# Unsplit float32 operands in the first block of a linear-attention and two-MLP kernel

## The chip, the cores and the metric

The kernel runs on one core of a Trainium2 chip. The metric is the device time of one execution in microseconds. Five engines work side by side, each through its own queue in order: TensorE (PE; its weight loads are listed as PEld), VectorE (DVE), ScalarE (ACT), GpSimd (POOL) and SyncE (SP), which here issues the DMAs.

## The reference

```python
def _attn_ref(q, k, v):              # 8 batches, 8 heads, 576 rows, 64 columns
    q_s = q - np.max(q, axis=-1, keepdims=True)
    q_s = np.exp(q_s)
    q_s = q_s / (np.sum(q_s, axis=-1, keepdims=True) + 1e-09)
    k_s = k - np.max(k, axis=2, keepdims=True)
    k_s = np.exp(k_s)
    k_s = k_s / (np.sum(k_s, axis=2, keepdims=True) + 1e-09)
    kv = np.einsum('bhsd,bhse->bhde', k_s, v)
    return np.einsum('bhsd,bhde->bhse', q_s, kv).astype(np.float32)

def _moe_ref(x, w_in, w_out):        # x 4608 x 512, w_in 512 x 2048, w_out 2048 x 512
    h = np.maximum(x @ w_in, 0.0)
    return (h * h @ w_out).astype(np.float32)

# the second MLP: h = x @ w_in;  g = h * (1 / (1 + exp(-h)));  g @ w_out
```

The output of the attention, 4608 rows of 512, goes through the first MLP and then through the second. Weights come as 64-bit floats.

## The kernel before, in words

Rows are handled in nine blocks of 512 for the first MLP: one for each batch's first 512 rows, and a ninth from the last 64 rows of all eight batches. The second MLP runs over six blocks of 768 rows.

Most products are made of "split" operands: `split` (L126) copies a float32 value to a rounded float32r part `hi` on ScalarE and subtracts it on VectorE to get `lo`; `mm3` (L195) multiplies hi by hi, hi by lo and lo by hi, three matmuls for one product. A few products use plain float32 operands: `kv` (L306) and the transposes `q_t` (L383).

The attention works on pairs of heads (`Pair`, L211), each in four phases (L434): maxima and exponents; subtraction, exponent of k and normalization of q; the product of k and v (`kvp`), the transposes of q and their split; the product of q with kv (`x`) and its evacuation. Batches 0 and 1 (`by_chunk = 2`, `natural`) lay rows out by chunk and reduce k over a strided axis (L279); the others use VectorE's transposes. Batch 0 is done before everything else (L716 to L760), its results split into `x0` at L424. The other batches are spread over the later work, one phase each time `next(attend)` is called.

The first block of the first MLP (L769 to L790) runs over 16 chunks f of the hidden width. In each, `h_mm` (L660) makes the first product of chunk f + 1 from `x0` and the weights of pair f // 2, `relu2` (L653) turns it into `g`, one attention phase is emitted, and `out_mm` (L672) adds chunk f to the second product `op`. Beside it the weights are converted from 64-bit words to float32 in `to_f32` (L146: two ScalarE and four VectorE operations) and split (`split_w`, L167), one half of a pair in each round: `o == 0` is the half of w_in, `o == 1` that of w_out. The float32 form of w_in is also stored (L174) for later.

The other eight blocks use Strassen-like products (`strassen`, L613): seven products per pair of chunks, of a left factor `wah`, `wal` (made by `make_wa`, L498, from the stored weights: a load, four VectorE operations, a split of 1792 columns, two stores) with seven combinations of x (class `X`, L540). A `Cache` (L473) holds two left factors; `want(t)` makes or loads those of the next uses. The first two are made at f = 14 (L782), followed by x of block 1.

Tiles of 8 KB per partition come from 19 shared slots through `take` and `give` (L81 to L90), oldest free slot first. A planner orders each engine's instructions ahead of time by its own estimates, so neighbouring steps are interleaved; `keep_in_program_order` keeps an instruction from moving ahead of earlier ones of its engine.

Of the kernel before, what the change touches and what calls it, by code (L numbers as in the profile page):

```python
# [10 lines left out]
F32 = mybir.dt.float32  # L11
F32R = mybir.dt.float32r
# [19 lines left out]
def kernel(  # L32
# [25 lines left out]
    NQ = 7  # L58
    TS = 768
    TH = TS // 2  # L60
    assert SM == TB and B * SL == TB and NB == B + 1 and SL <= P

    NP = NF // 2
    NS = 19
# [16 lines left out]
    def take(shape, dt, name):  # L81

        at = idle.pop(0)
        t = spool.tile(shape, dt, tag=f"s{at}", name=name)
        slot_of[id(t)] = (at, t)
        return t
# [5 lines left out]
    def f32(t):  # L92
        return t.bitcast(F32)
# [32 lines left out]
    def split(hi, lo, src):  # L126
        nc.scalar.copy(hi, src)  # L127
        nc.vector.tensor_sub(lo, src, f32(hi))  # L128
# [37 lines left out]

    def split_w(i, o, raw, pin=False):  # L167

        u = upool.tile([P, PW], U32, tag="u", name="u")
        to_f32(u, raw, pin)  # L170
        give(raw)
        yield
        if o == 0:
            nc.sync.dma_start(out=wf[0, i, o], in_=f32(u))  # L174
        W[i, o] = w = take([P, 2, PW], F32R, "w")
        split(w[:, 0], w[:, 1], f32(u))
        yield
# [17 lines left out]
    def mm3(ps, lh, ll, rh, rl, first, last):  # L195
# [2 lines left out]
        nc.tensor.matmul(ps, ll, rh, start=False, stop=last)  # L198


    x0 = [take([P, NK, TB], F32R, name) for name in ("xh", "xl")]
    XR = {}
    big = {}
    PLACES = {
# [4 lines left out]
    }  # L209

    class Pair:  # L211
# [64 lines left out]

        def k_max(self):
            m = self.tile("m", [P, 2, D], F32)
            r = nc.vector.reduce_max(m, self.kr.rearrange("p a c d -> p a d c"), axis=AX.X)  # L279
            if (self.b, self.p) == (1, 0):  # L280
                tc.keep_in_program_order(r)
            self.m = self.tile("mb", [P, 2, D], F32)
            nc.gpsimd.partition_all_reduce(
                self.m.rearrange("p a d -> p (a d)"), m.rearrange("p a d -> p (a d)"), P, bass_isa.ReduceOp.max
            )
# [28 lines left out]
        def kv_evac(self):  # L314
            rec = self.tile("rec", [P, 1], F32)
            nc.vector.tensor_scalar_add(rec, self.kvp[:, 2 * D:2 * D + 1], 1e-9)
            nc.vector.reciprocal(rec, rec)
            t = self.tile("m" if not self.early else "kvt", [P, 2 * D], F32)
            nc.vector.scalar_tensor_tensor(
                out=t, in0=self.kvp[:, 0:2 * D], scalar=rec, in1=mask_n if self.natural else mask_t,  # L320
                op0=ALU.mult, op1=ALU.mult,
            )
            self.kvh = self.tile("kvh", [P, 2 * D], F32R)
            self.kvl = self.tile("kvl", [P, 2 * D], F32R)
            nc.vector.tensor_copy(self.kvh, t)
            nc.vector.tensor_sub(self.kvl, t, f32(self.kvh))
# [69 lines left out]
                nc.vector.transpose(self.pt, self.q.rearrange("p c d -> p (c d)"))  # L396

        def q_split(self):
            self.qh = self.tile("qh", [P, S], F32R)
            self.ql = self.tile("ql", [P, S], F32R)  # L400
            if self.natural:
                split(self.qh[:, 0:SM], self.ql[:, 0:SM], self.pt[0])
                split(self.qh[:, SM:S], self.ql[:, SM:S], self.pt[1][:, 0:SL])
            else:
                split(self.qh, self.ql, self.pt)

        def x(self):
            ps = []
            for hf in range(2):
                xp = ps_a.tile([P, TB], F32, tag="pa", name="xp")  # L410
                s = slice(hf * HALF, (hf + 1) * HALF)
                mm3(xp[:, 0:HALF], self.kvh, self.kvl, self.qh[:, s], self.ql[:, s], True, True)
                ps.append(xp)
            self.xp = ps

        def x_evac(self):
            p, b = self.p, self.b
            if p == 0 and b > 0:
                XR[b] = take([P, NK, TB], F32, "xr")
            for hf, xp in enumerate(self.xp):  # L420
                n = HALF if hf == 0 else SM - HALF
                t0 = hf * HALF
                if b == 0:
                    split(x0[0][:, p, t0:t0 + n], x0[1][:, p, t0:t0 + n], xp[:, 0:n])  # L424
                else:
                    nc.scalar.copy(XR[b][:, p, t0:t0 + n], xp[:, 0:n])
                if hf == 1:
                    t = self.tile("xe", [P, SL], F32)
                    nc.scalar.copy(t, xp[:, n:n + SL])
                    nc.sync.dma_start(out=xld[p, :, b * SL:(b + 1) * SL], in_=t)  # L430
            if self.early:
                give(*(big[p, i] for i in range(3)))
# [40 lines left out]
    class Cache:  # L473
# [3 lines left out]
            self.n, self.uses, self.make, self.load = n, uses, make, load  # L477
            self.tiles, self.made = {}, set()

        def want(self, t):  # L480
            coming = list(dict.fromkeys(self.uses[t:]))
            for i in coming[:self.n]:
                if i in self.tiles:
                    continue
                if len(self.tiles) == self.n:
                    out = max(self.tiles, key=lambda x: coming.index(x) if x in coming else len(self.uses))
                    give(*self.tiles.pop(out))
                self.tiles[i] = (self.load if i in self.made else self.make)(*i)
                self.made.add(i)
# [170 lines left out]
    def h_mm(f):  # L660
        w = W[f // 2, 0]
        hp = ps_q.tile([P, TB], F32, tag="ac"[f % 2], name="hp")
        for c in range(NK):
            s = slice((f % 2 * NK + c) * P, (f % 2 * NK + c + 1) * P)
            mm3(hp, w[:, 0, s], w[:, 1, s], x0[0][:, c, :], x0[1][:, c, :], c == 0, c == NK - 1)
        if f % 2:
            give(W.pop((f // 2, 0)))
        return hp
# [103 lines left out]
    for f in range(NF):  # L772
        if f % 2 == 0 and f // 2 + 2 < NP:
            for o in range(2):
                raws.append(load_w(0, f // 2 + 2, o))
        if f + 2 < NF:
            run(split_w(f // 2 + 1, f % 2, raws.pop(0), pin=f == 0))
        if f + 1 < NF:
            G[f + 1] = first_g(f + 1)
        next(attend, None)  # L780
        if f == NF - 2:
            wa.want(0)  # L782
            xs = x_first(1)
            xs.split(2)
        elif f == NF - 1:
            give(*x0)
            xs.split(5)
        if f < NF - 2:
            run(out_mm(0, f // 2, f % 2, G.pop(f), f == 0, False))
# [3 lines left out]
    for j in range(1, NB):  # L793
        x, xs = xs, None
        for m, i in enumerate(turns[j - 1]):
            def hook(n):
                if n in (1, 6):
                    next(attend, None)
                    if j == 1 and (m, n) in ((1, 6), (3, 6)):
                        next(attend, None)  # L800
# [133 lines left out]
```

## Time and profile before

| what | us |
|---|---|
| median of 3 runs (lowest, highest) | 1693.26 (1692.67, 1694.72) |
| profiled execution, its own time | 1693.5 |
| its span in the profile | 1691.7 |
| mean granted TensorE clock | 0.994 of full |

Times in rows are microseconds from the start of the span, and mean durations of single instructions nanoseconds. L609 is line 609 of the kernel. A bracket at the end of a row is idle time of that engine just before it, with what ended it. Ends of matmuls are modelled, so the busy time of TensorE includes tails that overlap; the distance from start to start is the cost of one in a stream.

### The profile page before, as it was taken

The numbers are of one execution on the slowest core, as the hardware profiler recorded it, in microseconds if no ns is written. First come the engines' busy times: TensorE is split into PE (matmuls) and PEld (weight loads), VectorE is DVE, ScalarE is ACT, GpSimd is POOL, SyncE is SP. The second block draws the span as 40 slices with busy tenths as digits, with TensorE's granted clock in tenths as the row PEclk, the third lists the DMA queues.
The fourth block names the chain that finished last, engine by engine and source line by source line (L and its number), as shares of the span: only waits on it lengthen the run. The fifth ranks groups of instructions, "written<-read, shape, count | busy, mean of one in ns | idle before, by whom it ended". The sixth has DMA issues, their size and how long they took to land.

```text
span 1691.7 us, 23448 instructions
## 1 busy us (share of the span) xinstructions
PE 1633.6 (97%) x8904; PEld 1436.0 (85%) x8904; DVE 1015.5 (60%) x1723; ACT 868.2 (51%) x1551; POOL 55.5 (3%) x118
## 2 busy tenths in 40 slices
PE   4898999999999999999999999999999999999998
PEld 3676888888888888898988898899889889889887
DVE  7999888686776858653435675434444444444333
ACT  4876566565666656654546544334334334334332
POOL 1000000010101001000000000000000000000000
PEclk8999999999999999999999999999999999999999
DMA  7754667858576785746264875534534534534621
GB/s 210 253 196 159 190 210 220 260 160 256 177 236 193 208 242 166 250 146 237 109 215 171 332 280 196 188 131 167 196 132 158 196 141 149 196 150 149 218 94 38
DMA packets 193504, 320.31 MB, mean 189 GB/s; under 512 B 113264, under 2 KB 142960, under 8 KB 188528
## 3 DMA queue, kind: packets, MB, share of 16 engines
q1 hardware_dynamic: 193392, 318.81, 57.0%
q8 instruction: 70, 1.15, 0.3%
q14 instruction: 42, 0.34, 0.1%
HBM read 248.51 MB, written 70.25 MB: 188 GB/s over the span
## 4 chain that ended last, share of the span: by engine, by line
PE 72%; DVE 11%; ACT 5%; DMA 5%; issue 5%; SPq 1%; POOL 0%; POOLq 0%; DVEq 0%; ACTq 0%
PE a L609 18%; PE c L609 14%; PE y L197 8%; PE y L198 8%; PE y L196 8%; PE op L197 4%; PE op L196 4%; PE op L198 4%; DMA raw<-in_moe_w_out_dram 2%; DMA raw<-in_moe_w_in_dram 2%; PE kvp L310 1%; DVE u L160 1%; DVE g L128 1%; DVE u L163 1%; ACT raw L152 1%
## 5 line engine op out<-in xcount | busy, mean ns | idle before, releaser
L609 PE MATMUL a<-x,wah 128*128 128x256 f32 (+1 forms) x1792 | 398.0, 309 | 8.7 <-ACT h L646 4.4
L609 PEld LDWEIGHTS a<-x,wah 128*128 128x128 f32 x1792 | 314.9, 189 | 54.6 <-ACT h L646 9.7
L609 PE MATMUL c<-x,wah 128*128 128x256 f32 (+1 forms) x1344 | 296.3, 307 | 2.4 <-ACT h L624 1.8
L609 PE MATMUL a<-x,wal 128*128 128x256 f32 (+1 forms) x896 | 275.4, 307 | 0.6 <-DVE wal L128 0.5
L609 PEld LDWEIGHTS c<-x,wah 128*128 128x128 f32 x1344 | 237.9, 189 | 33.8 <-ACT h L624 3.8
L197 PE MATMUL op<-g,w 128*128 128x512 f32 x576 | 230.0, 399 | 2.9 <-DVE g L128 2.1
L196 PE MATMUL op<-g,w 128*128 128x512 f32 x576 | 224.2, 398 | 6.3 <-ACT g L127 3.9
L198 PE MATMUL y<-wb,g 128*128 128x512 f32 x576 | 227.2, 394 | 0.0
L197 PE MATMUL y<-wb,g 128*128 128x512 f32 x576 | 227.1, 394 | 0.0
L198 PE MATMUL op<-g,w 128*128 128x512 f32 x576 | 224.7, 392 | 0.0
L196 PE MATMUL y<-wb,g 128*128 128x512 f32 x576 | 223.5, 389 | 0.0
L609 PE MATMUL c<-x,wal 128*128 128x256 f32 (+1 forms) x672 | 206.6, 307 | 0.0
L870 ACT ACTIVATE z<-h 128x768 f32<-128x768 f32 x96 | 81.1, 846 | 227.8 <-DVE h L641 226.5
L632 DVE TENSOR_TENSOR h<-c,h 128x256 f32<-128x256 f32 (+1 forms) x112 | 53.6, 479 | 224.0 <-PE c L609 221.5
L609 PEld LDWEIGHTS a<-x,wal 128*128 128x128 f32 x896 | 169.3, 189 | 1.5 <-DVE wal L128 1.4
L654 ACT ACTIVATE h<-h 128x512 f32<-128x512 f32 x128 | 80.7, 630 | 119.9 <-DVE h L641 119.3
L128 DVE TENSOR_TENSOR g<-h,g 128x512 fp32r<-128x512 f32 x128 | 88.2, 690 | 78.2 <-ACT g L127 78.0
L871 DVE TENSOR_TENSOR z<-z,h 128x768 f32<-128x768 f32 x96 | 91.7, 957 | 68.5 <-ACT z L870 68.5
L198 PEld LDWEIGHTS y<-wb,g 128*128 128x128 f32 x576 | 107.9, 187 | 23.3
L609 PEld LDWEIGHTS c<-x,wal 128*128 128x128 f32 x672 | 127.2, 189 | 0.4
L198 PEld LDWEIGHTS op<-g,w 128*128 128x128 f32 x576 | 108.3, 188 | 21.7
L128 DVE TENSOR_TENSOR g<-z,g 128x768 fp32r<-128x768 f32 x96 | 91.6, 954 | 56.1 <-ACT g L127 56.1
(148 smaller groups left out, 2350.6 us busy)
## 6 DMA issues: line engine op xcount, KB each, us to landing
wah<-wad SPq DMA_DIRECT2D x72, 896.0 KB, 6.5
wal<-wad SPq DMA_DIRECT2D x72, 896.0 KB, 6.2
wb<-wbd SPq DMA_DIRECT2D x30, 1024.0 KB, 4.8
raw<-in_moe_w_in_dram SPq DMA_DIRECT2D x32, 512.0 KB, 5.3
raw<-in_moe_w_out_dram SPq DMA_DIRECT2D x32, 512.0 KB, 5.2
wad<-wah SPq DMA_DIRECT2D x16, 896.0 KB, 3.6
wad<-wal SPq DMA_DIRECT2D x16, 896.0 KB, 4.6
wf<-u SPq DMA_DIRECT2D x24, 512.0 KB, 4.9
```

The lines of the kernel that those rows point to most:

```text
L128: nc.vector.tensor_sub(lo, src, f32(hi))
L152: first = nc.scalar.activation(f32(lo32), lo32, AF.Copy, scale=2.0 ** -51, bias=2.0)
L160: nc.vector.scalar_tensor_tensor(out=u, in0=hi32, scalar=0x80000000, in1=u, op0=ALU.bitwise_and, op1=ALU.bitwise_xor)
L163: nc.vector.tensor_tensor(out=u, in0=u, in1=lo32, op=ALU.add)
L196: nc.tensor.matmul(ps, lh, rh, start=first, stop=False)
L197: nc.tensor.matmul(ps, lh, rl, start=False, stop=False)
L198: nc.tensor.matmul(ps, ll, rh, start=False, stop=last)
L609: nc.tensor.matmul(ps, l, r, start=first and c == 0 and n == 0, stop=c == 1 and n == 2, skip_group_check=True)
L632: nc.vector.tensor_add(h[:, 0, two], c, h[:, 0, two])
L654: nc.scalar.activation(h, src, AF.Relu)
L870: nc.scalar.activation(z, h, AF.Sigmoid)
L871: nc.vector.tensor_mul(z, z, h)
```

## The change

Four edits. In batches 0 and 1 the q and kv operands are not split: kv stays in one float32 tile, the transposed q is copied to one float32 tile, and each half of `x` is one float32 matmul. The results of batch 0 go unsplit to `XR[0]`, as those of the other batches do. Of the weights in the first block, those of w_in are converted into a shared slot and used unsplit by `h_mm`, one float32 matmul for each of four chunks in place of three of split operands; w_out is split as before. The k maxima of batches 0 and 1 are made by three `tensor_max` in place of one reduction. The first left factor is made at f = 12, the second inside the first Strassen block ahead of its fourth product.

```diff
@@ split_w
-        u = upool.tile([P, PW], U32, tag="u", name="u")
+        u = take([P, PW], U32, "w32") if o == 0 else upool.tile([P, PW], U32, tag="u", name="u")
         to_f32(u, raw, pin)
         give(raw)
         yield
         if o == 0:
             nc.sync.dma_start(out=wf[0, i, o], in_=f32(u))
+            W[i, o] = u
+            return
         W[i, o] = w = take([P, 2, PW], F32R, "w")
@@ before Pair
-    x0 = [take([P, NK, TB], F32R, name) for name in ("xh", "xl")]
-    XR = {}
+    XR = {0: take([P, NK, TB], F32, "xr")}
@@ Pair.k_max
-            r = nc.vector.reduce_max(m, self.kr.rearrange("p a c d -> p a d c"), axis=AX.X)
+            if self.natural:
+                t = self.tile("km", [P, 2, 2, D], F32)
+                nc.vector.tensor_max(t, self.kr[:, :, 0:2], self.kr[:, :, 2:4])
+                nc.vector.tensor_max(t[:, :, 0], t[:, :, 0], t[:, :, 1])
+                r = nc.vector.tensor_max(m, t[:, :, 0], self.kr[:, :, 4])
+            else:
+                r = nc.vector.reduce_max(m, self.kr.rearrange("p a c d -> p a d c"), axis=AX.X)
@@ Pair.kv_evac
+            if self.natural:
+                self.kv32 = t
+                return
             self.kvh = self.tile("kvh", [P, 2 * D], F32R)
@@ Pair.q_split
+            if self.natural:
+                self.q32 = self.tile("qh", [P, S], F32)
+                nc.scalar.copy(self.q32[:, 0:SM], self.pt[0])
+                nc.scalar.copy(self.q32[:, SM:S], self.pt[1][:, 0:SL])
+                return
@@ Pair.x
-                mm3(xp[:, 0:HALF], self.kvh, self.kvl, self.qh[:, s], self.ql[:, s], True, True)
+                if self.natural:
+                    nc.tensor.matmul(xp[:, 0:HALF], self.kv32, self.q32[:, s], start=True, stop=True)
+                else:
+                    mm3(xp[:, 0:HALF], self.kvh, self.kvl, self.qh[:, s], self.ql[:, s], True, True)
@@ Pair.x_evac
-                if b == 0:
-                    split(x0[0][:, p, t0:t0 + n], x0[1][:, p, t0:t0 + n], xp[:, 0:n])
-                else:
-                    nc.scalar.copy(XR[b][:, p, t0:t0 + n], xp[:, 0:n])
+                nc.scalar.copy(XR[b][:, p, t0:t0 + n], xp[:, 0:n])
@@ Cache
-        def want(self, t):
+        def want(self, t, n=None):
-            for i in coming[:self.n]:
+            for i in coming[:n or self.n]:
@@ h_mm
-            mm3(hp, w[:, 0, s], w[:, 1, s], x0[0][:, c, :], x0[1][:, c, :], c == 0, c == NK - 1)
+            nc.tensor.matmul(hp, f32(w[:, s]), XR[0][:, c], start=c == 0, stop=c == NK - 1)
@@ loop over f
-        if f == NF - 2:
-            wa.want(0)
+        if f == NF - 4:
+            wa.want(0, 1)
+        elif f == NF - 2:
             xs = x_first(1)
             xs.split(2)
         elif f == NF - 1:
-            give(*x0)
+            give(XR.pop(0))
@@ hook(n) of the Strassen blocks
+                if (j, m, n) == (1, 0, 3):
+                    wa.want(0)
```

## Rows read from the trace of the kernel before

**Rows 1.** The page: busy time of each engine and its share of the span.

```profile
PE 1633.6 (97%) x8904; PEld 1436.0 (85%) x8904; DVE 1015.5 (60%) x1723; ACT 868.2 (51%) x1551; POOL 55.5 (3%) x118
```

**Rows 2.** Busy by stretch: length, PE, PEld, DVE, ACT, POOL (instructions), clock, DMA, GB/s.

```profile
20.30:55.10 34.80, 26.94 (x108) 19.90 (x108) 30.55 (x67) 24.33 (x68) 1.16 (x3) 0.85 0.70 214
55.10:152.60 97.50, 91.94 (x414) 71.19 (x414) 95.23 (x139) 71.86 (x103) 9.96 (x15) 1.00 0.61 196
152.60:180.00 27.40, 21.55 (x100) 17.34 (x99) 25.43 (x50) 16.91 (x32) 1.01 (x3) 0.81 0.58 203
...
200.00:1691.70 1491.70, 1473.52 (x8163) 1310.23 (x8161) 835.98 (x1414) 736.88 (x1314) 36.26 (x64) 1.00 0.57 188
```

**Rows 3.** Busy time in three periods of the loop, kvp to kvp.

```profile
61.60:85.90 24.30, 22.85 (x105) 18.34 (x106) 24.07 (x38) 21.76 (x32) 3.24 (x4) 1.00 0.83 265
85.90:114.80 28.90, 26.88 (x121) 20.61 (x120) 27.72 (x38) 23.33 (x33) 2.99 (x4) 1.00 0.62 208
114.80:144.40 29.60, 28.12 (x127) 21.88 (x127) 28.98 (x41) 17.95 (x27) 2.72 (x4) 1.00 0.31 101
```

**Rows 4.** TensorE in order of time: start, length, instruction; ten starts, 58.80 to 60.90.

```profile
22.29 1.50 PE L310 MATMUL kvp<-big 128*128 128x129 f32 x6
...
29.04 0.83 PE L310 MATMUL kvp<-big 128*128 128x129 f32 x6
...
58.80 0.40 PE L198 MATMUL op<-g,w 128*128 128x512 f32 x1
...
60.90 0.40 PE L198 MATMUL op<-g,w 128*128 128x512 f32 x1
```

**Rows 5.** Line 310, 21.9 to 31.8 us: durations in ns, least, median, most.

```profile
L310 PE MATMUL kvp<-big x30: 272/422/583, 21.9 to 30.1; 128*128 128x129 f32 x24, 64*128 64x129 f32 x6
```

**Rows 6.** Groups of instructions, 0 to 200 us: busy us, mean ns, idle before.

```profile
L279 DVE TENSOR_REDUCE m<-kr 128x128 f32<-128x640 f32 x7 | 9.2, 1314 | 0.0
...
L127 ACT CAST wah<-c 128x1792 fp32r<-128x1792 f32 x4 | 6.8, 1693 | 2.2 <-DVE c L506 2.2
...
L338 DVE TENSOR_REDUCE qm<-q 128x10 f32<-128x640 f32 x4 | 3.2, 812 | 0.0
...
L128 DVE TENSOR_TENSOR ql<-qt,qh 128x512 fp32r<-128x512 f32 x4 | 2.8, 691 | 0.6 <-ACT qh L127 0.5
...
L326 DVE TENSOR_TENSOR kvl<-m,kvh 128x128 fp32r<-128x128 f32 x6 | 1.7, 284 | 0.0
...
L503 DVE TENSOR_TENSOR c<-c 128x256 f32<-128x256 f32 x4 | 1.6, 412 | 0.0
```

**Rows 7.** VectorE in order of time, start of the kernel.

```profile
36.16 0.45 DVE L128 TENSOR_TENSOR xl<-xp,xh 128x288 fp32r<-128x288 f32 x1
36.52 1.21 DVE L128 TENSOR_TENSOR w<-u,w 128x1024 fp32r<-128x1024 f32 x1
37.65 0.22 DVE L325 CAST big<-big 128x128 fp32r<-128x128 f32 x1
38.91 0.69 DVE L128 TENSOR_TENSOR big<-qt,big 128x512 fp32r<-128x512 f32 x1 [1.04 <-ACT big L127]
...
43.45 0.46 DVE L128 TENSOR_TENSOR xl<-xp,xh 128x288 fp32r<-128x288 f32 x1 [1.95 <-ACT xh L127]
```

**Rows 8.** TensorE in order of time, the first second product.

```profile
55.14 1.20 PE L196 MATMUL op<-g,w 128*128 128x512 f32 x4 [2.25 <-ACT g L127]
```

**Rows 9.** VectorE in order of time, change of stage.

```profile
157.25 2.02 DVE L128 TENSOR_TENSOR wal<-c,wah 128x1792 fp32r<-128x1792 f32 x1
...
161.33 0.68 DVE L128 TENSOR_TENSOR x<-xr,x 128x512 fp32r<-128x512 f32 x1
161.93 2.01 DVE L128 TENSOR_TENSOR wal<-c,wah 128x1792 fp32r<-128x1792 f32 x1
```

**Rows 10.** TensorE in order of time, the first Strassen product.

```profile
162.07 0.38 PE L609 MATMUL a<-x,wah 128*128 128x256 f32 x1 [1.79 <-DVE x L128]
```

**Rows 11.** SP's waits, 0 to 200 us: total, times, longest.

```profile
SPq L511 <- ACT wah L127: 6.1, 3, 2.3
```

More of the change, by code (lines that the diff above doesn't have):

```diff
@@ L60 @@
     TH = TS // 2
-    assert SM == TB and B * SL == TB and NB == B + 1 and SL <= P
+    assert SC == 4 and SM == TB and B * SL == TB and NB == B + 1 and SL <= P
     NP = NF // 2
@@ L398, in q_split @@
         def q_split(self):
+            if self.natural:
[3 more added lines that the diff above has]
+                return
             self.qh = self.tile("qh", [P, S], F32R)
             self.ql = self.tile("ql", [P, S], F32R)
-            if self.natural:
-                split(self.qh[:, 0:SM], self.ql[:, 0:SM], self.pt[0])
-                split(self.qh[:, SM:S], self.ql[:, SM:S], self.pt[1][:, 0:SL])
-            else:
-                split(self.qh, self.ql, self.pt)
+            split(self.qh, self.ql, self.pt)
         def x(self):
@@ L422, in x_evac @@
                 t0 = hf * HALF
-                if b == 0:
-                    split(x0[0][:, p, t0:t0 + n], x0[1][:, p, t0:t0 + n], xp[:, 0:n])
-                else:
-                    nc.scalar.copy(XR[b][:, p, t0:t0 + n], xp[:, 0:n])
+                nc.scalar.copy(XR[b][:, p, t0:t0 + n], xp[:, 0:n])
                 if hf == 1:
```

4 rows, old and new, of the table PLACES are left out of this document.

## The prediction

> **What bounds the kernel now.** I read the busy table of the page first, then the stretches of the first 200 us, then single instructions. TensorE is busy 97% of the span [rows 1], but that busy time includes its modelled pipeline tails, so I look for the stretches where it is not fed. There are three [rows 2]: 20.3 to 55.1 us (the attention of batch 0 and the first conversion; TensorE 26.9 of 34.8 us busy, mean clock 0.85), 55.1 to 152.6 us (the loop over f, 14 rounds of one first product and one second product), and 152.6 to 180 us (the change to the Strassen blocks; 21.6 of 27.4 us, clock 0.81). Behind 200 us TensorE is fed (1473.5 of 1491.7 us) and the change removes nothing, so I price that stretch at 0; the shared tile slots rotate in another order there, for which I keep 2 us on either side.
>
> In the loop VectorE, not TensorE, sets the pace. One period of four rounds (one head pair of attention, four weight conversions) took 28.9 and 29.6 us in the second and third period, with VectorE busy 27.7 and 29.0 us [rows 3]. TensorE's own work in a period is smaller. A split product of 512 columns starts every (60.90 - 58.80)/9 = 0.23 us [rows 4], so a round's 12 + 12 of them are 5.52 us, four rounds 22.1. A head pair adds ten kvp instructions at (0.83 - 0.272)/5 = 0.111 us [rows 4, 5], with a restart between chunks about 1.25; five transposes of the same rate, 0.55; and six xp matmuls of 288 columns at 0.13, scaled from the 512 (0.8). Together 24.7 us: 4 to 5 us of each late period are waits.
>
> **The change part by part, float32 on TensorE.** In the trace one float32 matmul in the code is two instructions: ten kvp for the five chunks. At full clock they start 0.111 us apart, at half clock (1.50 - 0.42)/5 = 0.216 us [rows 4, 5] (one lasts 0.27 or 0.42 us); for 129 columns that is two column times each (258 cycles of 1.2 GHz are 0.215 us). A second reading is one column time plus 128 columns of weights; 129 columns can't tell the two apart. Against it: the split products also load 128 weight columns for each matmul, and at 0.23 us for 512 columns (0.213 at one per cycle) nearly nothing of that shows. I take two column times per instruction: 512 columns cost 0.43 us, a chunk 0.86, a first product 4 x 0.86 = 3.45 us where 12 x 0.23 = 2.76 stood. Bounds for one first product: 2.13 us (the second reading, 8 x 640 columns) and 3.52 (8 x 512/129 x 0.111). The Trainium skill (FP8 and Floating Point Precision, TensorE Precision Notes) counts four passes for true FP32, which speaks against trading three split passes for it; by that rule the product is 3.4 us, by the second reading 2.1, and no run here yet shows float32 at 512 columns.
> Two float32 xp matmuls are 4 x 0.245 = 1.0 us for 0.8. A period of TensorE becomes 4 x (3.45 + 2.76) + 1.25 + 0.55 + 1.0 = 27.6 us.
>
> **VectorE and ScalarE relief.** Consecutive instructions overlap by about 0.08 us (a 1.21 us subtraction starts 1.13 us before the next [rows 7]), so I take means less 0.08 [rows 6]. Out of a period go: two weight subtractions 2 x 1.13 = 2.26; the q subtractions 0.61 + 0.14 (the 64-column one by the 128-column kvl less a third); kvl 0.20 and its copy, 0.13 by the same row; and 0.49 of the k maxima (the strided reduction 1.23, in its place one 256-element operation 0.33 and two of 128 at 0.20). That is 3.83 us, leaving 24 to 25 of 28 to 29. ScalarE loses two casts per period and is no bound (71.9 of 97.5 us [rows 2]).
> For the maxima the trace decides against a rule. The strided reduction takes 1314 ns, a reduction of as many elements along the row 812 [rows 6]: the layout costs 0.5 us, and it leaves with the reduction. The Trainium skill (VectorE: DVE Perf Modes, The TRN2 errata) says each small instruction pays its fixed part again. By its formula for two-operand adds, (N + 151)/0.96, taken for all four, one 640-element operation is 0.82 us and the three 1.01, an estimated loss of 0.2 per pair where the rows give a gain of 0.49.
>
> **The loop, 55.1 to 152.6.** After the change TensorE (27.6) is over VectorE (24 to 25), so TensorE bounds it: 3.5 periods are 96.6 us, and I add 3 us of waits. The nearest row for that is the first period, in which VectorE still had conversions done ahead: 24.3 us for about 24.7 of TensorE work [rows 3]. Sum 99.6 against 97.5: **+2**. Bounds: -0.5 (0.4 of waits) and +10 (today's 97.5 - 3.5 x 24.7 = 11 of waits stay).
>
> **The start, 20.3 to 55.1.** For the four pairs of batch 0 and the first weights VectorE loses 4 x (0.49 + 0.75 + 0.33), the subtractions of x (4 x 0.66: 0.36 by the starts at 36.16 and 36.52 [rows 7], and 0.3 for the shorter half) and one weight subtraction 1.13: 10.1 us. With them go its waits on ScalarE's copies, 1.04 and 1.95 [rows 7]; the first second product now starts at 55.14 after 2.25 us of waiting for g [rows 8]. If all of VectorE's time is on the path the gain is 13 us. TensorE gets 2 x 0.69 + 0.8 = 2.2 us more, partly at half clock, and the second conversion is emitted one round earlier, where ScalarE can stand before its data (0 to 3 us), so the other bound is +2. VectorE is busy 30.6 of 34.8 us [rows 2], which is nearer to the full gain, but the loads, TensorE and the chain through pair 3 share the path: I take half, **-6**.
>
> **The change of stage, 152.6 to 180.** Two left factors are made here now, each one 512 KB load, four VectorE operations (4 x 0.34), a ScalarE cast (1.69), a VectorE subtraction (1.94) and two 896 KB stores [rows 6, 9]. Both subtractions (157.25, 161.93) stand between the operations that make x [rows 9], and TensorE waits for x, 1.79 us at 162.07 [rows 10]. The first factor moves two rounds up: its 3.3 us of VectorE lie under the loop's 3 us per period of new slack; uncovered they would cost 3.3. The second moves behind all of x. Its load and stores stand in SP's order before the k, q and v loads of the pair after next, and SP already stands at such stores (6.1 us in three waits [rows 11]); those loads are used a block later, so I price that at 0, up to 2. The seven splits of x come about 4 us sooner, limited by the attention's output and the four subtractions ahead; TensorE's half-clock stretch behind the wait shrinks, 3; VectorE enters without its backlog, 1; and the second factor then costs its 3.3 us before the second block, of which I count 2. **-6**. Bounds: -12 (all waiting in these 27.4 us) and +9 (below). The POOL maxima stay as they are.
>
> **Sum.** -6 + 2 - 6 = -10 against the profiled execution's own 1693.5 us (span 1691.7, 1.8 around it), which lies 0.2 above the median 1693.26: **1683**.
>
> **The rivals.**
> 1. The waits of the loop stay (+10): they come from the chain from one product through ScalarE and VectorE to the next, not from VectorE's total. For it: at 55.14 TensorE waits for ScalarE's g, not for a busy VectorE. Against: the first period has no such waits. With -6 at the start and -4 at the change of stage it is 1693: no change that can be told.
> 2. Slower: the second factor is late. Place: between the first and second Strassen block, some 165 to 185 us. It can start only when VectorE has left x and the attention in front of it; four operations, cast and subtraction are 1.34 + 1.69 + 1.94 = 5 us in line [rows 6, 9], and if TensorE falls to half clock again, some 8 us of products lose 4 more. Then this stretch is +9 and the sum -6 + 2 + 9 = +5: 1698. It decides from +7.4 on in this stretch. For it: VectorE is busy in nearly all of it; against: TensorE still has second products to fill with.
> 3. Much faster: float32 goes by the second reading (loop back to VectorE's 24 to 25 per period, -10 to -12), or start and change of stage recover nearly all their waiting. 1671.
> 4. The change doesn't show: the planner orders the instructions so that the freed time becomes idle time on VectorE. 1693, counted with 1.
>
> **How the numbers follow.** Forecast 1683 (its own range 1677 to 1689.5): 0.56. Rivals 1 and 4: 0.20. Rival 2: 0.14. Rival 3: 0.10. The measurement can tell about 0.2%, 3.4 us. Faster is the forecast and rival 3: 0.66; same 0.20; slower 0.14. The range leaves out most of rival 2 and the far side of rival 3: 1673 to 1695.
>
> **What would show it.** Right: hp in 128 instructions 0.43 us apart at full clock; the first op near 49 us; periods of 28 to 29 us with VectorE under 26 busy; the first product of the blocks without the 1.8 us wait and its factor stored two rounds before. Wrong: hp spacing near 0.27 (rival 3), periods over 30 (rival 1), TensorE waiting for the second wal behind the first block (rival 2).

## The result

The changed kernel takes 1673.03 us (median of 4 runs, 1669.79 to 1675.97) beside 1692.97 for the kernel before on the same chip: a ratio of 0.9883, 95% interval 0.986 to 0.9905, or 20 us less. The forecast was 1683: faster, as it said, but by twice as much. The time lies at the very edge of the range that was given, 1673 to 1695, and outside the forecast's own, 1677 to 1689.5.

The page of the kernel after, its first line (against [rows 1]), and its granted clock in 40 slices:

```profile
PE 1632.9 (98%) x8824; PEld 1420.0 (85%) x8824; DVE 993.3 (59%) x1691; ACT 861.2 (51%) x1543; POOL 50.8 (3%) x118
...
PEclk9999999999999999999999999999999999999999
```

TensorE is as busy as before (1632.9 and 1633.6 us), in a span that is 17.5 us shorter: what has gone is waits. Busy by stretch, with the columns of [rows 2] (length, PE, PEld, DVE, ACT, POOL with instructions, clock, DMA, GB/s): start, loop over f, first Strassen step, and what lies behind the third:

```profile
17.10:46.10 29.00, 24.75 (x91) 16.57 (x92) 22.41 (x44) 21.96 (x72) 3.85 (x7) 1.00 0.61 180
46.10:149.00 102.90, 99.41 (x354) 61.67 (x353) 95.15 (x151) 72.61 (x105) 6.94 (x15) 1.00 0.72 230
149.00:163.60 14.60, 13.48 (x80) 11.24 (x79) 12.55 (x19) 9.95 (x19) 1.01 (x3) 1.00 0.57 169
...
188.30:1669.40 1481.10, 1470.95 (x8153) 1309.61 (x8153) 831.14 (x1408) 735.46 (x1312) 33.48 (x63) 1.00 0.56 187
```

The start is 6 us shorter and begins 3 us sooner, the loop is 5 us longer, and the change of stage (last first product to the end of the first Strassen step) takes 14.6 us where it took 24.1 (152.6 to 176.7). The clock, 0.85 and 0.81 in two stretches of [rows 2], is 1.00 in all of these (1.00 is 2.4 GHz; the traces show one other level, half of it). Three periods of the loop, as in [rows 3]:

```profile
51.90:83.30 31.40, 30.73 (x104) 18.20 (x103) 31.01 (x46) 25.40 (x36) 1.83 (x5) 1.00 0.84 283
83.30:111.30 28.00, 28.00 (x100) 17.55 (x99) 27.63 (x40) 23.11 (x32) 1.70 (x4) 1.00 0.95 299
111.30:140.90 29.60, 28.09 (x100) 17.55 (x99) 26.17 (x40) 16.36 (x26) 2.40 (x3) 1.00 0.48 158
```

The second and third are 28 and 29.6 us, as forecast. The first, 31.4, is not a period like them: by its instructions it holds 40 of the first product where they hold 32. TensorE in order of time at the first second product, and at the end of the loop:

```profile
42.25 4.46 PE L676 MATMUL hp<-xr,w 128*128 128x512 f32 x10
46.14 1.03 PE L198 MATMUL op<-g,w 128*128 128x512 f32 x2
...
146.41 3.17 PE L676 MATMUL hp<-xr,w 128*128 128x512 f32 x7
149.42 1.13 PE L424 MATMUL xp<-qh,m 128*128 128x288 f32 x4
150.17 0.62 PE L620 MATMUL a<-x,wah 128*128 128x256 f32 x2
```

Seven float32 instructions from 146.41 to 149.42 are 0.430 us each: the price of the forecast's first reading (0.43). The first second product starts without a wait (2.25 us in [rows 8]), and so does the first Strassen product at 150.17. (Before, the row of [rows 10] is that product's second instruction; the first ran at 157.11, and then the product waited 1.79 us for x.) VectorE at the start and at the factors, which are to be set against [rows 9]:

```profile
0.81 0.06 DVE L102 MEMSET tiny<- 128x1 f32 x1 [0.81 <-PEq L932]
3.63 0.42 DVE L282 TENSOR_TENSOR big<-big 128x256 f32<-128x256 f32 x1 [2.76 <-DMA big<-in_k_dram]
4.09 0.29 DVE L283 TENSOR_TENSOR big<-big 128x128 f32<-128x128 f32 x1
6.89 0.42 DVE L282 TENSOR_TENSOR big<-big 128x256 f32<-128x256 f32 x1 [2.51 <-DMA big<-in_k_dram]
7.35 0.29 DVE L283 TENSOR_TENSOR big<-big 128x128 f32<-128x128 f32 x1
11.10 0.29 DVE L284 TENSOR_TENSOR big<-big 128x128 f32<-128x128 f32 x1 [3.45 <-DMA raw<-in_moe_w_in_dram]
...
15.45 0.42 DVE L282 TENSOR_TENSOR big<-big 128x256 f32<-128x256 f32 x1
15.78 0.21 DVE L379 RECIPROCAL big<-big 128x10 f32<-128x10 f32 x1
15.91 0.28 DVE L283 TENSOR_TENSOR big<-big 128x128 f32<-128x128 f32 x1
16.11 0.82 DVE L381 TENSOR_TENSOR qn<-big 128x640 f32<-128x640 f32 x1
...
17.58 0.28 DVE L284 TENSOR_TENSOR big<-big 128x128 f32<-128x128 f32 x1
17.77 0.81 DVE L348 TENSOR_REDUCE big<-big 128x10 f32<-128x640 f32 x1
...
131.81 2.02 DVE L128 TENSOR_TENSOR wal<-c,wah 128x1792 fp32r<-128x1792 f32 x1
...
153.63 2.02 DVE L128 TENSOR_TENSOR wal<-c,wah 128x1792 fp32r<-128x1792 f32 x1
```

For pairs 0 and 1 two of the three maxima now run between 3.63 and 7.64, from the landing of their first part of k on; before, VectorE's first operation on data, a strided reduction, began at 10.43. GpSimd in the kernel before, that reduction, and GpSimd after the change:

```profile
10.19 0.20 POOL L253 MEMSET big<- 64x128 f32 x1
```

```profile
10.43 1.24 DVE L279 TENSOR_REDUCE big<-big 128x128 f32<-128x640 f32 x1 [9.56 <-POOL big L253]
```

```profile
10.86 0.20 POOL L254 MEMSET big<- 64x128 f32 x1
```

The reduction did not wait for a load: both loads of k of pair 0 had landed by 4.05 us. It waited for GpSimd, which fills the padding rows of the fifth chunk of k (L253) only after its masks, until 10.39. The first two maxima don't read that chunk and need not wait for it; the third does, as the reduction did, and starts at 11.10, just behind the memset (the bracket of its row names a load that landed shortly before it). No run moved the memset itself forward, so what that would give is open. The first factor's subtraction stands 25 us sooner than in the kernel before, the second's 8.

### The profile page after: what moved, and what is told of

It is laid out like the page before. It is cut to its first block, busy times and chain, and to the rows that moved or that the text cites. A ratio compares the mean times of both kernels' runs of the same rounds, so it can differ in the third digit from the quotient of the medians.

```text
span 1674.2 us, 23234 instructions
## 1 busy us (share of the span) xinstructions
PE 1632.9 (98%) x8824; PEld 1420.0 (85%) x8824; DVE 993.3 (59%) x1691; ACT 861.2 (51%) x1543; POOL 50.8 (3%) x118
## 4 chain that ended last, share of the span: by engine, by line
PE 62%; DVE 2%; ACT 2%; DMA 2%; issue 1%; POOL 0%; DVEq 0%; POOLq 0%; ACTq 0%; SPq 0%
PE a L620 16%; PE c L620 12%; PE y L199 8%; PE y L200 8%; PE y L198 8%; PE op L199 3%; PE op L198 3%; PE op L200 3%; PE kvp L317 0%; DMA x1d<-o 0%; ACT h L665 0%; DMA raw<-in_moe_w_in_dram 0%; DMA raw<-in_moe_w_out_dram 0%; DMA c<-wf 0%; ACT h L666 0%
## 5 line engine op out<-in xcount | busy, mean ns | idle before, releaser
L620 PEld LDWEIGHTS c<-x,wah 128*128 128x128 f32 x1344 | 237.1, 188 | 31.8 <-ACT h L635 3.1
L200 PEld LDWEIGHTS op<-g,w 128*128 128x128 f32 x576 | 108.3, 188 | 21.9
```

The costliest lines, as they stand in the source:

```text
L620: nc.tensor.matmul(ps, l, r, start=first and c == 0 and n == 0, stop=c == 1 and n == 2, skip_group_check=True)
```

## The experiments

The kernels are compared by their times and by five points of their traces: first transpose (qt), first second product (op), last first product (hp), end of the first and of the third Strassen step; and by the length from there to the last product of the second MLP. Times are medians; ratios are to the kernel before, run beside each.

| kernel | us | ratio, interval | qt | op | last hp | step 1 | step 3 | behind |
|---|---|---|---|---|---|---|---|---|
| before | 1692.97 | 1 | 20.3 | 55.1 | 152.6 | 176.7 | 201.0 | 1486.0 |
| after | 1673.03 | 0.9883, 0.9860–0.9905 | 17.1 | 46.1 | 149.0 | 163.6 | 188.3 | 1481.1 |
| product_only | 1679.56 | 0.9923, 0.9906–0.9941 | 20.8 | 49.9 | 152.4 | 165.4 | 191.2 | 1478.4 |
| qkv_only | 1686.37 | 0.9963, 0.9948–0.9978 | 21.2 | 52.7 | 146.7 | 168.2 | 192.5 | 1485.0 |
| kmax_only | 1692.60 | 1.0003, 0.9991–1.0014 | 16.3 | 51.8 | 149.9 | 173.9 | 198.2 | 1486.5 |
| factor_only | 1697.26 | 1.0034, 1.0021–1.0048 | 20.1 | 54.2 | 151.8 | 174.6 | 200.0 | 1496.7 |
| after_no_factor | 1673.09 | 0.9881, 0.9862–0.9901 | 16.9 | 45.9 | 148.5 | 161.9 | 186.9 | 1482.0 |
| after_no_kmax | 1679.72 | 0.9922, 0.9908–0.9937 | 20.7 | 47.9 | 152.5 | 167.2 | 191.9 | 1481.5 |
| after_no_qkv | 1683.83 | 0.9952, 0.9938–0.9967 | 16.9 | 50.2 | 149.3 | 162.6 | 187.6 | 1488.2 |
| before_pe_more | 1689.45 | 0.9977, 0.9959–0.9996 | 20.7 | 55.2 | 159.0 | 174.0 | 198.3 | 1485.4 |
| before_dve_more | 1699.95 | 1.0052, 1.0034–1.0069 | 21.2 | 55.3 | 162.3 | 185.3 | 209.6 | 1483.6 |
| after_pe_more | 1689.52 | 0.9983, 0.9969–0.9997 | 16.7 | 44.0 | 160.0 | 174.6 | 199.7 | 1478.3 |
| after_dve_more | 1685.18 | 0.9955, 0.9939–0.9971 | 16.2 | 43.4 | 145.5 | 160.1 | 184.4 | 1491.8 |
| before_fill | 1693.22 | 1.0010, 0.9998–1.0023 | 21.1 | 52.5 | 152.8 | 177.2 | 204.2 | 1480.6 |

Runs of one kernel lie up to 2 to 8 us from their median, so a point of one trace is good to a few us. Some traces are of runs at the edge: factor_only's took 1703.2 us, the longest of 12, after_pe_more's 1684.6, the shortest of 10, and the changed kernel's 1676.0, the longest of 4.

### One part alone

**product_only**: the kernel before with the float32 first product and its operands.

```diff
-            mm3(hp, w[:, 0, s], w[:, 1, s], x0[0][:, c, :], x0[1][:, c, :], c == 0, c == NK - 1)
+            nc.tensor.matmul(hp, f32(w[:, s]), XR[0][:, c], start=c == 0, stop=c == NK - 1)
```

> The first block's first product alone in float32 on unsplit operands (weights of w_in and x of block 0 unsplit); q and kv split, k maxima by the reduction, both left factors at f = 14, as before. Theory 1 (VectorE's relief is worth what it frees at the start and at the change of stage, while the loop is given to TensorE): start -4, loop +4 to +6 (14 x 0.69 more TensorE work, VectorE near 26 per period), change of stage -2, in all -2: 1691, between 1688 and 1695. Theory 2 (most of the change's 20 us is TensorE's clock, which stays full once this product no longer waits for VectorE's subtractions): the granted clock is 1.00 through 30 to 60 us, and the time is 1685 or less.

It gave 12 us, not 2 (1679.56 beside 1691.83). What theory 2 asked for came true, a clock of 1.00 through 30 to 60 us and a time under 1685; but VectorE's relief came with it; the section on the clock looks at the clock by itself. The loop is 102.5 us, as after the change, and the change of stage 13.0 with both factors called where they were before. Its loop and first Strassen step:

```profile
49.90:152.40 102.50, 99.15 (x359) 61.73 (x359) 98.11 (x151) 72.04 (x103) 8.75 (x15) 1.00 0.71 234
152.40:165.40 13.00, 12.02 (x78) 10.45 (x77) 12.68 (x29) 9.55 (x20) 1.05 (x3) 1.00 0.32 96
```

The planner had put both subtractions of the left factors into the loop by itself, at 140.6 and 145.3 us, into the time that VectorE no longer needs:

```profile
140.59 2.02 DVE L128 TENSOR_TENSOR wal<-c,wah 128x1792 fp32r<-128x1792 f32 x1
...
145.29 2.02 DVE L128 TENSOR_TENSOR wal<-c,wah 128x1792 fp32r<-128x1792 f32 x1 [0.55 <-ACT wah L127]
```

VectorE has 10.8 us less to do in the change of stage (12.68 for 23.46), and the stretch is 11.1 us shorter. The two factors are about 5 of these; splits of x and work of the attention, which also stand elsewhere now, are the rest.

**qkv_only**: q, kv and `x` of batches 0 and 1 unsplit, nothing else.

```diff
-                mm3(xp[:, 0:HALF], self.kvh, self.kvl, self.qh[:, s], self.ql[:, s], True, True)
+                if self.natural:
+                    nc.tensor.matmul(xp[:, 0:HALF], self.kv32, self.q32[:, s], start=True, stop=True)
+                else:
+                    mm3(xp[:, 0:HALF], self.kvh, self.kvl, self.qh[:, s], self.ql[:, s], True, True)
```

> q with kv alone in float32 in batches 0 and 1; everything else as before. Theory 1: VectorE loses 1.08 us in each of eight pairs, 4.3 at the start and 4.3 in the loop, where it sets the pace, TensorE gains 0.2 per pair: -4 to -7, 1687 to 1690. Theory 2 (clock): less than -2 unless the clock of 30 to 50 us rises.

5.5 us less (1686.37 beside 1691.83), as the sum for this part said: loop 94.0 us (3.5 shorter: TensorE does not bound it here and VectorE has less), start 3.3 shorter, measured from the first transpose.

**factor_only**: `want(0, 1)` at f = NF - 4 and the second `want(0)` in the first Strassen step.

```diff
-        if f == NF - 2:
-            wa.want(0)
+        if f == NF - 4:
+            wa.want(0, 1)
+        elif f == NF - 2:
             xs = x_first(1)
```

> The first left factor at f = 12 and the second inside the first Strassen block; everything else as before. Theory 1 (the move pays only under the loop's slack): 3.3 us of VectorE are added to a loop that VectorE bounds, +3, and 5 are gained at the change of stage: -2, 1691. Theory 3 (the place alone pays: x is no longer behind two factors, TensorE does not wait and its clock does not fall): -6 to -10 with the granted clock 1.00 through 160 to 180 us.

Slower by 5.4 us (1697.26 beside 1691.83), which neither theory had. Up to the third step it is 1.0 us ahead; the loss comes behind, 1496.7 us for 1486.0 (see the last part of this section). Moving the factor in a kernel whose VectorE has no free time before the change of stage moves the end of the first step by 2 us.

**after_no_factor**: the changed kernel with both factors made at f = 14 as before.

```diff
-        if f == NF - 4:
-            wa.want(0, 1)
-        elif f == NF - 2:
+        if f == NF - 2:
+            wa.want(0)
             xs = x_first(1)
```

> The changed kernel with both left factors at f = 14 again. Theory 1: the change of stage is some 5 to 6 us longer than in the changed kernel, 1678 to 1680. Theory 3: 8 to 10 us longer, 1681 to 1683, with the clock falling in 150 to 180 us. If neither (under 2 us): the 10 us at the change of stage came from VectorE entering it without backlog.

1673.09: the move is worth nothing in the change, which is the third case of the expectation (VectorE enters the change of stage without a backlog). The subtractions of both factors stand at 137.0 and 138.9 us without it.

**kmax_only** and **after_no_kmax**: the maxima by halves alone, and the change without them.

```diff
+                nc.vector.tensor_max(t, self.kr[:, :, 0:2], self.kr[:, :, 2:4])
+                nc.vector.tensor_max(t[:, :, 0], t[:, :, 0], t[:, :, 1])
+                r = nc.vector.tensor_max(m, t[:, :, 0], self.kr[:, :, 4])
```

> The kernel before with the maxima of k of the first two batches by halves, alone. Theory of the forecast (0.49 us of VectorE per pair, eight pairs, VectorE being the pace up to 152 us): start 2 us sooner, loop 1 to 2 shorter, time down by 2 to 4. Theory 2 (the first maximum can start when the first half of k has landed, as the trace after the change shows with its first VectorE operation at 3.6 us in place of 10.4): first transpose at 17, down by 4 to 6. By the Trainium skill (VectorE: DVE Perf Modes, The TRN2 errata), which has each small instruction pay its fixed part: up by 0 to 2.

> The changed kernel with the maxima of k by one strided reduction again. Theory 2 (the maxima by halves bring the first transpose 3 us forward): first transpose at 20 to 21, first op at 49, time up by 2 to 5 against the changed kernel (1675 to 1678). Theory of the forecast (only 0.49 us per pair, and the loop is bound by TensorE now): up by 1 to 2.

Alone no change can be told in the time (1692.60 beside 1691.71, where the two theories had 2 to 6 us less; only the third forecast, up by 0 to 2, fits the time), though the trace is 4.0 us ahead at the first transpose and 2.8 at the third step. In the changed kernel the medians differ by 6.7 us, more than any theory said and clear of noise, and the traces by 3.6 at the third step and 4.0 in all. So the edit brings the first transpose forward by 3 to 4 us, of which 3 or so are left at the third step. Why the time shows nothing of it in one kernel and more in the other stays open.

**after_no_qkv**: the change with q and kv split.

```diff
-                self.q32 = self.tile("qh", [P, S], F32)
+                split(self.qh[:, 0:SM], self.ql[:, 0:SM], self.pt[0])
+                split(self.qh[:, SM:S], self.ql[:, SM:S], self.pt[1][:, 0:SL])
```

> The changed kernel with q and kv of batches 0 and 1 split again (two subtractions and one copy more for q and kv of each pair on VectorE, 1.08 us a pair; x by three split matmuls, 0.2 us a pair less on TensorE). Theory 1 (only VectorE's work ahead of the loop still counts, since TensorE is the pace in the loop): first op 2 to 4 us later than 46.1, loop within 2 us of 103, time up by 2 to 4 against the changed kernel (1675 to 1678). Rival (the edit is worth as much here as alone, where it gave 6 us): 1678 to 1681. If TensorE's 0.2 us a pair decides: within 1 us of the changed kernel.

First op 4.1 us later, as theory 1 said (2 to 4), but the loop is 3.8 shorter (99.1), and the third step ends 0.7 sooner than in the changed kernel: the 8.5 us that this part gives alone up to there (201.0 to 192.5) are not to be had a second time once the product has relieved VectorE. The time is 10.8 us longer all the same, more than any of the three expectations, and the trace shows where: it is 7.1 us longer behind the third step.

### Which engine sets the pace of the loop

Four kernels add the same kind of work to before and after. On TensorE the first of the four products of `h_mm` is repeated (its sum is begun anew), once after and four times before the change, about 0.9 us a round; on VectorE the clip of a conversion is repeated (it finds nothing left to clip), 0.61 us a round.

```diff
+            if c == 0 and f:
+                nc.tensor.matmul(hp, f32(w[:, s]), XR[0][:, c], start=True, stop=True)
```

```diff
-        nc.vector.tensor_scalar(
-            out=f32(u), in0=f32(u), scalar1=EXP_LO, scalar2=EXP_HI, op0=ALU.max, op1=ALU.min
-        )
+        for _ in range(1 + more):
+            nc.vector.tensor_scalar(
+                out=f32(u), in0=f32(u), scalar1=EXP_LO, scalar2=EXP_HI, op0=ALU.max, op1=ALU.min
+            )
```

**after_pe_more**

> The changed kernel with more TensorE work in the loop over f and no other: in rounds 1 to 15 the first of the four float32 products of h_mm is issued twice (the second one starts the sum anew), two instructions of 0.43 us, so 0.86 us a round, 12 us over the 14 rounds between the first second product and the last first product. Theory 1 (after the change TensorE is the pace of the loop): that stretch goes from 103 to 112 to 115 us, the time up by 9 to 13. Rival (the pace is still VectorE or the chain through ScalarE and VectorE): stretch up by under 4 us, time up by 0 to 5.

**after_dve_more**

> The changed kernel with more VectorE work in the loop and no other: the clip of each converted half pair behind the first pair is issued twice (the second finds nothing to clip), one instruction of 0.69 us, 0.61 from start to start, 8.5 us over 14 rounds. Theory 1 (TensorE is the pace, VectorE has slack): the stretch stays within 3 us of 103, the time within 4. Rival (VectorE is still the pace): stretch and time up by 6 to 9.

**before_pe_more**

> The kernel before with the extra work on TensorE: in rounds 1 to 15 the first split product of h_mm is issued five times in place of once (each starts the sum anew), 4 x 0.23 = 0.92 us a round, 13 us over 14 rounds. Theory 1 (before the change VectorE sets the pace and TensorE has 4 to 5 us a period to spare): the stretch goes from 97.5 to 98 to 102 us, time up by 0 to 4. Rival (TensorE, or a chain in which its time counts, is the pace): up by 10 to 13.

**before_dve_more**

> The kernel before with the extra clip on VectorE, 0.61 us a round, 8.5 us over 14 rounds. Theory 1 (VectorE sets the pace before the change): stretch and time up by 6 to 9. Rival (the waits of a period belong to a chain of latencies, not to VectorE's total): up by 0 to 3.

The loop of after_pe_more, after_dve_more, before_pe_more and before_dve_more, one line each:

```profile
44.00:160.00 116.00, 111.56 (x382) 66.97 (x381) 96.90 (x152) 72.71 (x105) 10.42 (x15) 1.00 0.64 205
```

```profile
43.40:145.50 102.10, 99.74 (x353) 61.40 (x352) 99.63 (x154) 72.36 (x104) 7.38 (x15) 1.00 0.72 231
```

```profile
55.20:159.00 103.80, 103.78 (x470) 84.67 (x471) 102.24 (x151) 76.10 (x106) 12.30 (x15) 0.97 0.60 196
159.00:174.00 15.00, 13.54 (x83) 11.40 (x82) 14.85 (x31) 10.07 (x21) 1.01 (x3) 1.00 0.57 202
```

```profile
55.30:162.30 107.00, 95.96 (x414) 72.97 (x414) 103.24 (x150) 72.86 (x104) 9.18 (x15) 0.97 0.55 176
162.30:185.30 23.00, 16.31 (x83) 13.18 (x82) 22.85 (x45) 14.18 (x24) 1.01 (x3) 0.85 0.52 202
```

After the change, 12 us of TensorE work lengthen the loop by 13.1 and 8.5 us of VectorE work by -0.8. Before it, 8.5 us of VectorE work cost 9.5, and 13 us of TensorE work 6.3 (up to 4.5 expected): the rest found room in TensorE's waits, until TensorE was busy in all of the loop (103.78 of 103.80 us). The pace has passed from VectorE to TensorE. The times of whole kernels say this less well: after_pe_more is 16.5 us slower than the changed kernel (9 to 13 expected), and after_dve_more 12.2 (at most 4 expected), though it is ahead by 3.9 us at the third step; it loses them all behind it.

The second line of before_pe_more shows more. It stands against this one of the kernel before, the same stretch:

```profile
152.60:176.70 24.10, 18.70 (x83) 14.91 (x82) 23.46 (x45) 13.96 (x25) 1.01 (x3) 0.79 0.55 210
```

Nothing was changed in this stretch, and yet the first Strassen step ends 15.0 us after the last first product in place of 24.1, the clock stays at 1.00, and the kernel with 13 us more work is 3.6 us faster than the kernel before (1689.45 beside 1693.02; the interval, 0.9959 to 0.9996, ends close to 1). With the loop 6 us longer, VectorE has 31 instructions and 14.85 us left in this stretch, where it had 45 and 23.46. What VectorE does in this stretch is nearly all of its length: 23.46 of 24.1 us, 22.85 of 23.0, 14.85 of 15.0, 12.68 of 13.0 in product_only. After the change it is 12.55 of 14.6, and TensorE, busy 13.48 us, is nearer to the bound.

### The clock

**before_fill**: the kernel before with products of the identity with itself, meant for the waits of TensorE and overwritten by the products that follow.

```diff
+    def fillers(ps, n):
+        for _ in range(n):
+            nc.tensor.matmul(ps[:, 0:P], ident, ident, start=True, stop=True)
...
+                if self.early and self.p < 2:
+                    fillers(xp, 2 if hf else 5)
...
+        fillers(a, n[0])
         product(a, w, A11, x[0], True)
```

> The kernel before with TensorE kept busy in its waits: float32 products of the identity with itself (two instructions of 0.11 us each at full clock), whose results are overwritten, ahead of kvp of pairs 1 and 2 and of x of pairs 0 and 1 (20 products, 4.4 us), and ahead of the first, second and sixth product of the first two Strassen steps (37 products, 8 us). Theory 1 (the fall of the clock is a consequence of the waits and costs little by itself, since TensorE waits for VectorE anyway): the granted clock stays at 1.00 or nearly, the first op stays within 2 us of 55, the time within 4 us of before. Theory 2 (the half clock itself costs: 20.5 us of it before, up to 10 us of work): with the clock at 1.00 the time falls by 5 to 10. If the added products lie on the path: up by 3 to 12.

Start, loop and first Strassen step:

```profile
21.10:52.50 31.40, 24.79 (x129) 19.02 (x129) 30.47 (x68) 24.32 (x68) 1.22 (x3) 0.90 0.75 228
52.50:152.80 100.30, 93.43 (x413) 72.36 (x414) 95.30 (x138) 72.10 (x103) 10.00 (x15) 0.98 0.60 190
152.80:177.20 24.40, 20.80 (x129) 18.43 (x128) 24.25 (x47) 14.13 (x26) 1.02 (x3) 0.93 0.58 218
```

The half clock at 33.3 to 43.6 us is gone and the start is 3.4 us shorter, but the loop gives all of it back (its last first product is at 152.8, before at 152.6): VectorE has 95.3 us to do in it. But the edit did not do in the start what it was made for. The planner ran half of the start's added products ahead of the first transpose:

```profile
9.68 3.35 PE L197 MATMUL xp<-ident 128*128 128x128 f32 x14 [9.68 <-POOL ident masks.py:199]
12.82 1.25 PE L197 MATMUL kvp<-ident 128*128 128x128 f32 x6
21.06 1.11 PE L394 MATMUL qt<-ident,qn 128*128 128x128 f32 x4 [7.00 <-DVE qn L377]
```

In the 7.00 us of idle time behind them the clock fell, and it stayed at half from 17.1 to 27.3 us. In all, the half clock lasts 17.0 us up to the third step where it lasted 20.5. So theory 1's time came (1693.22), but not its condition, a clock of 1.00 or nearly, and it can't price the clock in the start. Another run gives a hint there: the start of kmax_only has the same 108 instructions on TensorE and not one at half clock, and is no shorter than the 34.8 us of the kernel before:

```profile
16.30:51.80 35.50, 25.97 (x108) 19.51 (x108) 31.67 (x74) 26.10 (x78) 4.62 (x8) 1.00 0.73 217
```

It begins 4 us sooner, so not all of its waits are the same. In the change of stage before_fill did what it was made for: the half clock lasts 3.4 us in place of 10.2, and the stretch is as long as before, with VectorE busy 24.25 of 24.4 us. So beside the waits for VectorE the half clock costs nothing that can be seen here. The added products take TensorE time themselves, so a small cost of the clock could hide behind them.

### Behind the third step

The code behind the third step is the same in all these kernels, and yet its length goes from 1478.3 to 1496.7 us in the traces. The order in which the planner put the instructions there is not the same. I compared the sequences of TensorE's products by their names in the traces with those of the kernel before, in three pieces: the rest of the first Strassen block, blocks 2 to 4, blocks 5 to 8. In the second MLP behind them the order is the same in all, and its length too, 764.4 to 765.3 us.

- The same order in all three pieces (qkv_only, kmax_only, before_pe_more, before_dve_more and the kernel before): 1483.6 to 1486.5 us; the first piece is 63.3 or 63.4 in all five.
- Another order in the first piece, nearly the same in the second, the same in the third (the changed kernel, product_only, after_no_factor, after_no_kmax, after_pe_more, and before_fill but for its own products): 1478.3 to 1482.0; the first piece is 60.6 to 61.3.
- Another order in all three (factor_only, after_dve_more, after_no_qkv): 1488.2 to 1496.7; the first piece is 63.5 to 66.4.

The first piece goes with the order closely. The other two pieces do not: in the five traces with one order throughout, blocks 2 to 4 take 291.0 to 294.5 us and blocks 5 to 8 362.5 to 365.7; in the third group they take 291.8 to 299.0 and 364.5 to 369.3. Part of the 18 us is also the choice of the traced runs. If each length is set right by the difference between its traced run and its kernel's median, the groups are 1484 to 1488, 1478 to 1483 and 1488 to 1494 us: still some 5 us apart from middle to middle, but their edges touch. The line of factor_only, whose traced run was 6 us longer than its median:

```profile
200.00:1696.70 1496.70, 1476.03 (x8154) 1308.25 (x8153) 834.31 (x1413) 737.46 (x1314) 38.03 (x63) 1.00 0.56 187
```

Against the changed kernel's line above, the busy time is 5 us more and the idle time 10.5. This is where factor_only, after_dve_more and after_no_qkv lose the 6 to 16 us by which they are slower than their first 200 us say. It is a match of 14 traces; no run changed the order alone, so the cause is not shown, and what in an edit makes the planner take one order or another stays open.

## Why the prediction was right and wrong

**The sum.** From trace to trace the parts of the gain are -3.2 us ahead of the first transpose, -5.8 in the start, +5.4 in the loop, -9.5 in the change of stage, +0.4 in the second and third step and -4.9 behind them: -17.6. The medians add 2.4, since the changed kernel's trace is of the longest of its runs. Of the 10 us that the forecast was short, about 8 lie in places that it priced at nothing (ahead of the first transpose and behind 200 us), and its loop and change of stage are each off by 3.5, in opposite ways.

**Float32 at 512 columns: right.** 0.430 us per instruction against 0.43, so 0.86 a chunk. The Trainium skill (FP8 and Floating Point Precision, TensorE Precision Notes) counts four passes for FP32; the trace agrees: 0.86 us is 3.7 times the 0.23 of one split product [rows 4].

**The start, -6: right number, by a guess.** From first transpose to first second product 34.8 us became 29.0. The forecast took half of what VectorE and its waits could give, and no run shows that share: product_only has this stretch at 29.1 us although VectorE is busy 27.88 us in it, only 2.7 less than before, so its length doesn't follow VectorE's total. What it missed lies in front: it began its sum at 20.3 us, and the first transpose came 3.2 us sooner. It priced the maxima by their length alone (0.49 us a pair; from start to start they take 0.33 + 0.20 + 0.19 = 0.72, where the reduction took 1.15, so that was nearly right) and not by when they can run. The reduction reads the padding rows, which GpSimd fills by 10.39 us; two of the three maxima don't. The Trainium skill's fixed part per instruction (VectorE: DVE Perf Modes, The TRN2 errata) gives by its formula for two-operand adds an estimated 0.42, 0.29 and 0.29 us for the three maxima; the trace agrees, with 0.42, 0.29 and 0.29. The loss of 0.2 us that was estimated from it comes from taking the same formula for the reduction, 0.82 us; here the strided reduction takes 1.24.

**The loop, +2: right engine, term too small.** It is +5.4. TensorE's work was right (14 rounds and the attention of the stretch are 97.1 us by starts, forecast 96.6), but 6 us of it are waits and not 3. The 3 came from the first period of [rows 3], read as "24.3 us for about 24.7 of TensorE work". The row's own count says otherwise: x105 where the later ones have x121 and x127; only 36 products of op fell into it, not 48. Its work was 21.8 us and its waits 2.5 per period, which would have put 9 in the loop. The row was not a full period. The later two hold 51 and 57 products of op, so that about 3 us of each are waits, and not 4 to 5.

**The change of stage, -6: right direction for the wrong reason, and too small.** It was -9.5 (24.1 to 14.6). The forecast laid 4 us of it to moving the factor behind x and to the two rounds by which the first moves up, 3 to the clock, 1 to "VectorE enters without its backlog". The runs turn this about: without the move nothing changes (after_no_factor), with the move alone 2 us (factor_only), and the same 9 us come from giving VectorE more time before it (before_pe_more) or less work (product_only, 11). By these runs the backlog was nearly the whole term, and it stood there at 1. Rival 2, the late second factor, did not occur: the subtraction stands at 153.6 us, and TensorE does not wait for it.

**The clock, 3 of the -6**: no gain of its own could be found (before_fill in the change of stage).

**Behind 200 us, 0 within 2: wrong.** It is 4.9 us shorter behind the third step. The step that failed is that equal code takes equal time: its length goes with the planned order, by some 5 us from group to group here, though no run shows that the order is the cause.

**The parts don't add up.** Alone they are worth -12.3, -5.5, +0.9 and +5.4 us by the medians. Up to the third step the product gives 9.8, q and kv 8.5, the maxima 2.8, and all together 12.7: each of the first two takes away the same wait for VectorE, and then TensorE is the bound. The rivals: 1 (waits of the loop stay, 11 us) is half right in the loop, where 6 stay, and was outweighed. 3 named about the right time, 1671, for its second half (start and change of stage recover nearly all waiting), but largely by luck: the change of stage recovered 9.5 of the 12 us that the forecast thought possible, the start 5.8 of 13, and some 8 us came from places that no rival named.

## What to carry to other kernels

When an engine that sets the pace of a loop is relieved, count what it carries out of the loop: here its backlog set the length of the next stage (23.46 of 24.1 us), and the planner moved work into the freed time by itself. When an engine waits, look up what the last writer of its operand was: here a reduction stood behind a memset of padding rows on another engine, and not behind a load. Before a period of a trace is taken as a yardstick, compare its instruction count with its neighbours'. An edit to planned code can come with another order of work far behind it, and lengths there differed by some 5 to 10 us between groups of orders here, so an edit's effect is read at the points of the trace near it and the whole only with several variants. And look where added work ran before its run is taken as a test: half of the products that were to fill waits in the start ran before it.

## What was not expected of the hardware

Adding 13 us of TensorE work to the kernel before made it 3.6 us faster (ratio 0.9977, 0.9959 to 0.9996). A start with the granted clock at full (kmax_only, 35.5 us) was no shorter than one with 10.3 us at half clock (34.8), and taking the half clock from 10.2 to 3.4 us in the change of stage left its length as it was (24.1 and 24.4 us).
